# First queries from raw weights, constants inside the planned order, a weight bound by a broadcast product, and transfers counted in flight: one change to a pre-norm transformer block

## The chip, the cores and the metric

The kernel runs on one core of one Trainium2 chip. The metric is the device time of one execution in microseconds (us); lower is better. A core has TensorE (PE in the profile, its weight loads PEld), VectorE (DVE), ScalarE (ACT), GpSimd (POOL) and SyncE (SP), which here only issues transfers. Each engine works through its own instructions in program order and waits where an instruction needs another engine's result.

## The reference

A pre-norm block over one sequence of 2048 tokens of width 640: attention with 32 heads of 20 in a sliding window of 256 keys, then a gated feed-forward of width 1536. All arrays are float32.

```python
def _layernorm(x, axis=-1, eps=1e-5):
    m = jnp.mean(x, axis=axis, keepdims=True)
    v = jnp.var(x, axis=axis, keepdims=True)
    return (x - m) / jnp.sqrt(v + eps)

def _A_ref(x, wqkv, wo):
    H = 32; Dh = D // H; W = 256
    qkv = (x @ wqkv).reshape(B, S, 3, H, Dh).transpose(2, 0, 3, 1, 4)
    q, k, v = qkv[0], qkv[1], qkv[2]
    scores = jnp.einsum("bhqd,bhkd->bhqk", q, k) * (Dh ** -0.5)
    mask = (idx[:, None] - idx[None, :] >= 0) & (idx[:, None] - idx[None, :] < W)
    p = softmax(where(mask, scores, -1e9))
    o = jnp.einsum("bhqk,bhkd->bhqd", p, v)
    return o.transpose(0, 2, 1, 3).reshape(B, S, D) @ wo

def _B_ref(x, w_gate, w_up, w_down):
    return (gelu(x @ w_gate) * (x @ w_up)) @ w_down

h = x + _A_ref(_layernorm(x), wqkv, wo)
h2 = h + _B_ref(_layernorm(h), w_gate, w_up, w_down)
```

## The kernel before

**Precision.** A product of two fp32 matrices is made of three fp16 products: each operand is scaled by a power of two and split into a high and a low half (`xh`, `xl`; `w0h`, `w0l` for the query weights, `w1` for the keys', `w2` for the values'), and high x high, high x low and low x high are summed in PSUM. The power of two of a weight is a bound on its absolute values. `Weight.scale` makes it: a sum or maximum of absolute values per partition into `am`, a product on TensorE that brings all partitions' values to every partition (through `dg`, the identity times `am`, against a matrix of ones), a maximum on VectorE, and bit operations for `pw` (the power) and `sw` (its inverse). `Weight.split` writes the high halves on ScalarE, and `low` the low halves on VectorE.

**Tiles and stages.** The tokens are 16 blocks of 128 and 8 chunks of 256 (two blocks). A block is normalised (`layernorm`, VectorE with a power on GpSimd), transposed on TensorE against `ident`, and split into `xh` and `xl`. `qk(c, 0)` and `qk(c, 1)` make the queries and keys of chunk c: five feature tiles of 128, each a sum over five slices of the inner dimension, three fp16 matmuls of 256 columns for each. Two feature tiles share a PSUM bank (`mm`, two of them); `qk_out` splits the result, writes both halves to DRAM (tile `qk`), and `stack` reads them back into `qT` and `kT`, six transfers each, in the layout in which one matmul covers all three half products of a head pair. Maxima of each row come first (`maxima`, TensorE into `ra` or `rb`, then VectorE into `junk` and `mxs`), then the scores, the exponentials on ScalarE, the windows' edges on GpSimd, and the values on TensorE (`pv`). The output projection, the second normalisation and the feed-forward follow; parts of them run beside the attention of later blocks.

**Storage in the start.** The raw query weights lie in the two buffers that become `qT`; the raw key weights lie in `gu`, which later holds split gate and up weights; blocks 1 to 3 of the input lie in buffers of `pt`. SP issues, in this order: blocks 0 and 1, the five slices of the query weights (`qT<-in_wqkv_dram`), those of the keys (`gu<-in_wqkv_dram`), block 2, the value weights, blocks 3 and 4, then the first slices of the output weights (`wsl`).

**The order of the work.** Nothing is placed by hand. Each piece of work is a generator (a lane); it yields the engine that it needs next and a function that tells when its operands are ready. `Clock` keeps a modelled time for each engine and tile, with a cost for each instruction (`Engine.cost`) and each transfer (`Clock.issue`). The loop at the end looks at the lanes in a fixed preference and emits the next instruction of the first one that can start by the modelled time. So what is emitted, and in what order each engine gets it, follows from the modelled times; on the chip an engine keeps to that order, and waits where its model was too early. When nothing can be emitted and no score has been made yet, a matmul of the fp16 identity into `pv` is emitted, which computes nothing that is used:

```python
            if not pos["score"] and nc.t["tensor"] <= now:
                nc.tensor.matmul(pv[:, 0, :], ident16, ident16, start=True, stop=True)
```

The list order holds from `tc.manual_schedule()` on, which stands just ahead of that loop; what was emitted before it (the identities, the ones, the mask, the memset of `pv`) is placed by the framework's own scheduler.

**What the change touches.** `scale_lane` runs `Weight.scale` for one weight; the keys' waits until the queries' scale is emitted, the values' until the keys' is. `split_lane` splits in the order queries, keys, values, and so on. `big_lane` writes constants into rows of `kT` on GpSimd (12 memsets) once the queries' scale is emitted. `x_lane` normalises and transposes the blocks; from block 2 on it waits for the keys' scale. `dense_lane` picks the next dense product; `can` says whether it may start. In the modelled transfer before, each engine's transfers queue up behind one another (`moved`), and land 3.0 or 3.2 after their last byte was moved:

```python
            self.moved[eng] = max(self.moved[eng], start + 0.2) + cost * (1.2 if run <= 512 else 1)
            end = self.moved[eng] + (3.0 if eng == "sync" else 3.2)
```

Of the kernel before, what the change touches and what calls it, by code (L numbers as in the profile page):

```python
# [53 lines left out]
class Clock:  # L54

    LAT = 0.18
    NOW = ("tensor", "vector", "scalar", "gpsimd", "sync")

    def __init__(self, nc):
        self.nc = nc
        self.t = dict.fromkeys(self.NOW, 0.0)
        self.wr, self.rd, self.rings = {}, {}, {}
        self.warm, self.win, self.use = False, 0, 0.0
        self.mode, self.half = "full", 0
        self.moved = dict.fromkeys(self.NOW, 0.0)
        for e in self.NOW:
            setattr(self, e, Engine(self, e))
# [90 lines left out]
    def issue(self, eng, cost, reads, writes, move=None):  # L160
        start = self.t[eng]
        boxes = [self.box(a) for a in reads], [self.box(a) for a in writes]
        for a, (k, b) in zip(reads, boxes[0]):
            start = max(start, self.latest(self.wr, k, b, eng))
            if a.space == PSUM:
                start = max(start, self.others(a, eng))
        for k, b in boxes[1]:
            start = max(start, self.latest(self.wr, k, b, eng), self.latest(self.rd, k, b, eng))
        if move:
            run = min(b[4] for a, (_, b) in zip(reads + writes, boxes[0] + boxes[1])  # L170
                      if a.space != DRAM)
            self.t[eng] = start + (move if run > 512 else 0.7)
            self.moved[eng] = max(self.moved[eng], start + 0.2) + cost * (1.2 if run <= 512 else 1)
            end = self.moved[eng] + (3.0 if eng == "sync" else 3.2)
        else:
            end = self.t[eng] = start + cost
        for k, b in boxes[0]:
            self.note(self.rd, k, b, eng, end)
        for k, b in boxes[1]:
            self.note(self.wr, k, b, eng, end)  # L180


class Engine:
# [23 lines left out]
    def cost(self, op, out, ins):  # L207
        n = out.free_size()
        if op.startswith("dma_start"):
            size = n * out.partition_size() * mybir.dt.size(out.dtype)  # L210
            return size / (300e3 if mybir.dt.size(out.dtype) == 4 else 150e3)
        half = mybir.dt.size(out.dtype) == 2 and ins and mybir.dt.size(ins[0].dtype) == 2
# [31 lines left out]
def block_kernel(ctx: ExitStack, tc: tile.TileContext, x, wqkv, wo, wg, wu, wd, out):  # L244
# [70 lines left out]


    ident = const.tile([P, P], F32, name="ident")
    nc.vector.memset(ident, 1.0)
# [14 lines left out]
    class Weight:  # L333
# [35 lines left out]
        def scale(self, lane, tp="tp"):  # L369
# [17 lines left out]

            dg = nc.tile(lnp, [P, P], F32, "dg")
            yield on("vector", am)
            nc.vector.tensor_scalar(dg, ident, am[:, 7:8], _pow2(-self.e), op0=ALU.mult, op1=ALU.mult)  # L390
            yield pe(dg, slots=[tp])
            t = bank(tp)
            nc.tensor.matmul(t[:, 0:P], ones, dg, start=True, stop=True)
            pc = pw[:, self.col:self.col + 1]
# [177 lines left out]
    rooms = {"k": gu.bitcast(F32)[:, :KC * D].rearrange("p (c f) -> p c f", f=D)}  # L572
    rooms["k"] = [rooms["k"][:, i] for i in range(KC)]
    gu = gu.rearrange("p (a c f) -> p a c f", c=KC, f=512)

# [36 lines left out]
    esc = const.tile([P, 1], F32, name="esc")  # L612
    hsc = const.tile([P, 1], F32, name="hsc")

    def qk_scale():
# [13 lines left out]
    class Block:  # L629
        ready = False  # L630
        maxima = halves = v = 0
        h, turned, normed = None, False, False
        scored = normal = wrote = 0
# [13 lines left out]
    def x_lane(blocks, lane):  # L647

        for j in blocks:
            c = C[j // 2]  # L650
            if j > 1:
                yield on("vector", when=lambda: W["k" if j < NR else "v"].scaled)
            if j >= NR and j + 1 < NB:
                yield ("sync",), lambda: max(0.0, nc.slot(att, "xt", 2))
                load_x(j + 1)

            def dst():
                if c.x is None:
                    c.x = tuple(nc.tile(wq, [P, KC, CW], F16, n, 3) for n in ("xh", "xl"))
                return tuple(t[:, :, B[j].cols] for t in c.x)  # L660

            yield from layernorm(B[j].x, lane, None, None, dst,
                                 lambda: j < 6 or c.x or C[j // 2 - 3].used == 4,
                                 lambda: B[j].x, tp="rb" if j in (1, 3) else "tp")
            B[j].ready = True

# [8 lines left out]
    def qk(c, which):  # L675

        w = W["qk"[which]]
        xh, xl = C[c].x
        wh, wl = w.hl
        d = dram.tile([2, D, CW], F16, name=f"qk{c}{which}")  # L680
        left = [3]
        for t0 in range(0, KC, 2):
# [11 lines left out]
    def qk_out(c, which, ts, ps, d, left):  # L694

        o = ps[:, :len(ts) * CW].rearrange("p (t n) -> p t n", n=CW)
        yield on("scalar", ps, when=lambda: pos["qk"] < pos["qks"] + 2)
# [5 lines left out]
        nc.vector.scalar_tensor_tensor(lo, o, _pow2(QE), hi, op0=ALU.mult, op1=ALU.subtract)  # L703
        done("mm")
# [618 lines left out]
    def scale_lane(todo, lane):  # L1323
        for i in todo:
# [36 lines left out]
    def dense_lane():  # L1361
# [96 lines left out]

    ctx.enter_context(tc.manual_schedule())
    class Lane:  # L1460
# [11 lines left out]
        def start(self, now):  # L1472
# [43 lines left out]
    while dense.alive or sides or side or outs or tasks:  # L1516
# [8 lines left out]
        ahead = pos["dense"] / DENSE - pos["score"] / (H // 2) - TARGET  # L1525
        early = [l for l in sides if l.gen.__name__ == "x_lane"] if not B[XF].ready else []
        if not W["v"].ready:
# [71 lines left out]
```

## Time and profile before

| | |
|---|---|
| median of 3 runs | 1050.79 us |
| the three runs | 1049.81, 1050.79, 1056.80 us |
| the profiled execution's own time | 1054.5 us |
| its span in the trace | 1052.8 us |
| mean granted TensorE clock | 0.995 of full speed |
| TensorE busy | 1022.7 us, 97% of the span |
| VectorE busy | 777.7 us, 74% |
| ScalarE busy | 489.3 us, 46% |
| GpSimd busy | 266.5 us, 25% |
| first matmul that computes something of the queries | at 22.20 us |
| first matmul of the attention's maxima that waited for keys | at 63.60 us |
| matmuls of the identity into `pv` | 424, until 106.7 us |

Almost every instruction is issued through one helper, so all have line 192 in the profile; groups are told apart by the tiles' names instead. In an instruction's row, `out<-in` are the program's tiles. In a timeline row the first two numbers are start and duration; rows of one kind that follow closely are merged, with their count behind an x, and brackets give the idle time of the engine just before and what ended it. In the chain of waits the columns are start, duration and what was running. In a table of windows each pair is an engine's busy time and number of instructions; behind the pairs stand the granted clock, the share of the DMA engines and GB/s.

### The profile page before, as it was taken

What the parts mean: (1) busy time and instruction counts of PE and PEld (TensorE: products, weight loads), DVE (VectorE), ACT (ScalarE), POOL (GpSimd) and SP (SyncE); (2) the same over time, 40 slices, a digit from 0 to 9 for tenths busy, and PEclk for the clock granted to TensorE, in tenths of its full rate; (3) what the DMA queues carried; (4) which work ended last, traced back from release to release, by engine and by line L of the source; (5) the groups of instructions that cost most, each with busy time, mean ns of one, the idle gap of its engine ahead of it and who ended that gap; (6) DMA issues with size and microseconds to landing.
All of it is one profiled execution on the core that took longest, in us unless ns stands there. A gap on an engine that the chain in (4) does not pass through costs nothing.

```text
span 1052.8 us, 27290 instructions
## 1 busy us (share of the span) xinstructions
PE 1022.7 (97%) x10966; PEld 697.9 (66%) x10966; DVE 777.7 (74%) x2196; ACT 489.3 (46%) x936; POOL 266.5 (25%) x367
## 2 busy tenths in 40 slices
PE   6999899999999999999999999999999999999998
PEld 6977566766766666666655564455777777777776
DVE  5678899998778777666778848576899976555553
ACT  5431566675666666656668763432221222222120
POOL 5000223223323323323334430113434410000000
PEclk9999989999999999999999999999999999999999
DMA  7462445534132231412232224132352471132211
GB/s 288 114 165 55 145 119 118 166 92 105 40 100 80 74 81 40 107 55 77 51 135 76 78 39 162 51 102 75 116 160 100 136 215 59 68 101 101 76 51 50
DMA packets 85727, 105.91 MB, mean 101 GB/s; under 512 B 22944, under 2 KB 59040, under 8 KB 84640
## 3 DMA queue, kind: packets, MB, share of 16 engines
q1 hardware_dynamic: 62496, 93.41, 29.9%
q10 hardware_dynamic: 23104, 10.75, 3.9%
q8 instruction: 86, 1.41, 0.6%
q14 instruction: 41, 0.34, 0.1%
HBM read 71.11 MB, written 28.84 MB: 95 GB/s over the span
## 4 chain that ended last, share of the span: by engine, by line
PE 81%; DVE 10%; ACT 3%; DMA 3%; issue 3%; POOL 1%; SPq 0%; ACTq 0%; DVEq 0%; POOLq 0%
PE mm L192 41%; PE pv L192 12%; PE ra L192 11%; PE rb L192 9%; PE tp L192 7%; DVE junk L192 3%; DMA kT<-qk 1%; ACT pt L192 1%; DMA qk<-qks 1%; DVE am L192 1%; DVE gel L192 0%; DVE gu L192 0%; ACT wst L192 0%; POOL ws L192 0%; DVE ht L192 0%
## 5 line engine op out<-in xcount | busy, mean ns | idle before, releaser
L192 POOL TENSOR_SCALAR_AFFINE_SELECT pt<-pt 128x512 f32<-128x512 f32 x240 | 153.3, 661 | 327.0 <-ACT pt L192 322.6
L192 DVE CUSTOM_DVE_ANT_0 junk<-ra,mask 128x384 bf16<-128x384 f32 (+2 forms) x264 | 140.1, 531 | 41.0 <-PE ra L192 20.9
L192 DVE CUSTOM_DVE_ANT_0 junk<-rb,mask 128x384 bf16<-128x384 f32 (+2 forms) x248 | 131.1, 529 | 43.3 <-PE rb L192 26.0
L192 ACT ACTIVATE pt<-rb,esc 128x384 f32<-128x384 f32 (+2 forms) x246 | 130.1, 581 | 67.3 <-PE rb L192 47.6
L192 ACT ACTIVATE pt<-ra,esc 128x384 f32<-128x384 f32 (+2 forms) x234 | 122.7, 575 | 77.7 <-PE ra L192 68.9
L192 PE MATMUL pv<-pt,v 128*21 128x128 f32 x2880 | 105.0, 277 | 1.0 <-ACT oT L192 0.8
L192 PEld LDWEIGHTS <-ah 128*128 128x128 f16 x768 | 74.9, 98 | 30.2 <-issue 2.9
L192 PEld LDWEIGHTS pv<-pt,v 128*21 128x21 f32 x2880 | 68.8, 101 | 16.0 <-issue 1.8
L192 ACT ACTIVATE gel<-gel,ffk 128x512 f32<-128x512 f32 x32 | 23.1, 722 | 121.0 <-DVE gel L192 116.5
L192 PEld LDWEIGHTS <-kT 62*128 62x128 f16 x1440 | 58.4, 95 | 21.4 <-issue 11.2
L192 ACT CAST ah<-gel 128x512 f16<-128x512 f32 x48 | 29.6, 617 | 82.6 <-DVE gel L192 81.0
L192 PEld LDWEIGHTS <-ws 128*128 128x128 f16 x640 | 62.6, 98 | 7.2
L192 DVE SCALAR_TENSOR_TENSOR ht<-mm,ffk,ht 128x320 f32<-128x320 f32 x96 | 52.0, 545 | 20.6 <-PE mm L192 18.5
L192 PEld LDWEIGHTS <-qT 60*128 60x128 f16 x640 | 24.7, 93 | 63.2 <-issue 59.2
L192 PEld LDWEIGHTS <-gu 128*128 128x128 f16 x440 | 41.8, 98 | 36.9 <-issue 1.5
L192 PE MATMUL mm<-xl,w0h 128*128 128x256 f16 x200 | 54.8, 274 | 0.0
L192 PE MATMUL mm<-xh,w0h 128*128 128x256 f16 x200 | 54.7, 274 | 0.0
L192 PE MATMUL mm<-xl,w1h 128*128 128x256 f16 x200 | 54.7, 273 | 0.0
L192 PE MATMUL mm<-xh,w1l 128*128 128x256 f16 x200 | 54.6, 273 | 0.0
L192 PE MATMUL mm<-xh,w1h 128*128 128x256 f16 x200 | 54.6, 273 | 0.0
L192 PE MATMUL mm<-xh,w0l 128*128 128x256 f16 x200 | 54.6, 273 | 0.0
L192 PE MATMUL mm<-w2h,xh 128*128 128x320 f16 x160 | 48.1, 300 | 0.6 <-DVE qks L192 0.6
(287 smaller groups left out, 2533.5 us busy)
## 6 DMA issues: line engine op xcount, KB each, us to landing
ws<-wsums SPq DMA_DIRECT2D x20, 640.0 KB
qk<-qks ACTq DMA_DIRECT2D x64, 128.0 KB
qT<-qk SPq DMA_DIRECT2D x48, 160.0 KB
kT<-qk SPq DMA_DIRECT2D x48, 160.0 KB
wsums<-ws SPq DMA_DIRECT2D x12, 640.0 KB
ht<-in_x_dram SPq DMA_DIRECT2D x16, 320.0 KB
h_dram<-ht SPq DMA_DIRECT2D x16, 320.0 KB
ht<-h_dram SPq DMA_DIRECT2D x16, 320.0 KB
```

Of the source, the lines that this page charges most:

```text
L192: r = real(*args, **kw)
```

## The change

- **First chunk's queries in fp32.** `qk(0, 0)` multiplies the raw fp32 query weights with the normalised, transposed, unsplit blocks 0 and 1 (new tile `x32`, which lies in `gu` behind the raw key weights), one fp32 matmul of 256 columns for each pair of feature tile and slice. It may start when both blocks are `full` and the query weights' transfers are issued; the power of two is applied in `qk_out` through `qs`. `x_cast` makes `xh` and `xl` of these two blocks afterwards (ScalarE, then GpSimd), once the keys' scale is emitted. The keys are split ahead of the queries, and the stacks of chunks 0 and 1 wait until the query weights are split.
- **Constants inside the list order.** `tc.manual_schedule()` moves ahead of the constants.
- **Weight bound by a broadcast product.** `am`'s column, scaled, is broadcast as the stationary operand against the identity; the diagonal `dg` goes.
- **Transfers in flight.** The order's model of a transfer changes: all engines' transfers share one line, a transfer waits until the eighth before it has landed, the rates and delays are others, and `SAFE` is added to each landing.

```diff
     LAT = 0.18
+    SAFE = 0.5
...
+        self.line, self.window = 0.0, deque(maxlen=8)
...
         if move:
+            if len(self.window) == self.window.maxlen:
+                start = max(start, self.window[0])
             run = min(b[4] for a, (_, b) in zip(reads + writes, boxes[0] + boxes[1])
                       if a.space != DRAM)
-            self.t[eng] = start + (move if run > 512 else 0.7)
-            self.moved[eng] = max(self.moved[eng], start + 0.2) + cost * (1.2 if run <= 512 else 1)
-            end = self.moved[eng] + (3.0 if eng == "sync" else 3.2)
+            self.t[eng] = start + (0.35 if run > 512 else 0.75)
+            out = writes[0].space == DRAM
+            self.line = max(self.line, self.t[eng] + (0.3 if out else 1.1)) + cost
+            end = self.line + (0.9 if out else 1.1) + self.SAFE
+            self.moved[eng] = self.line
+            self.window.append(end)
...
         if op.startswith("dma_start"):
-            size = n * out.partition_size() * mybir.dt.size(out.dtype)
-            return size / (300e3 if mybir.dt.size(out.dtype) == 4 else 150e3)
+            size = math.prod(c for _, c in out.ap) * mybir.dt.size(out.dtype)
+            if op == "dma_start_transpose":
+                return size / 150e3
+            wide = mybir.dt.size(out.dtype) == 4 or out.space == DRAM
+            return size / (380e3 if wide else 150e3)
...
+    ctx.enter_context(tc.manual_schedule())
     ident = const.tile([P, P], F32, name="ident")
...
-            dg = nc.tile(lnp, [P, P], F32, "dg")
             yield on("vector", am)
-            nc.vector.tensor_scalar(dg, ident, am[:, 7:8], _pow2(-self.e), op0=ALU.mult, op1=ALU.mult)
-            yield pe(dg, slots=[tp])
+            nc.vector.tensor_scalar(am[:, 7:8], am[:, 7:8], _pow2(-self.e), None, op0=ALU.mult)
+            yield pe(am, slots=[tp])
             t = bank(tp)
-            nc.tensor.matmul(t[:, 0:P], ones, dg, start=True, stop=True)
+            nc.tensor.matmul(t[:, 0:P], am[:, 7:8].to_broadcast([P, P]), ident, start=True,
+                             stop=True)
...
+    x32 = gu.bitcast(F32)[:, KC * D:KC * (D + CW)].rearrange("p (c n) -> p c n", n=CW)
...
             def dst():
-                if c.x is None:
-                    c.x = tuple(nc.tile(wq, [P, KC, CW], F16, n, 3) for n in ("xh", "xl"))
-                return tuple(t[:, :, B[j].cols] for t in c.x)
+                if j < 2:
+                    return x32[:, :, B[j].cols], None
+                return xparts(j)
...
-            B[j].ready = True
+            if j < 2:
+                B[j].full = True
+                tasks.append(x_cast(j))
+            else:
+                B[j].ready = True
+
+    def xparts(j):
+        c = C[j // 2]
+        if c.x is None:
+            c.x = tuple(nc.tile(wq, [P, KC, CW], F16, n, 3) for n in ("xh", "xl"))
+        return tuple(t[:, :, B[j].cols] for t in c.x)
+
+    def x_cast(j):
+        src = x32[:, :, B[j].cols]
+        yield on("scalar", src, when=lambda: W["k"].scaled)
+        hi, lo = xparts(j)
+        nc.scalar.copy(hi, src)
+        yield on("gpsimd", hi)
+        nc.gpsimd.tensor_tensor(lo, src, hi, op=ALU.subtract)
+        B[j].ready = True
...
+                if first:
+                    yield from products(KC, lambda k: [(w.raw[0, k][:, fs], x32[:, k, :])],
+                                        at_=(ps, i * CW))
+                    continue
...
+        up = qs if c == which == 0 else _pow2(QE)
+        yield on("scalar", ps, when=lambda: pos["qk"] < pos["qks"] + 2 and (c or pos["qs"]))
...
-        nc.scalar.activation(hi, o, AF.Copy, scale=_pow2(QE))
+        nc.scalar.activation(hi, o, AF.Copy, scale=up)
...
-        yield ("sync",), need(d, when=lambda: pos["big"] == 2 and (c < 2 or B[2 * c - 3].scored),
-                              eng="sync")
+        yield ("sync",), need(d, when=lambda: pos["big"] == 2 and (W["q"].ready if c < 2 else
+                                                                B[2 * c - 3].scored), eng="sync")
...
+            if i == 0:
+                yield on("vector", sw)
+                nc.vector.tensor_scalar(qs, sw[:, C_Q:C_Q + 1], _pow2(QE), None, op0=ALU.mult)
+                pos["qs"] = 1
...
-        for i, w in enumerate(weights):
+        for i, w in [(1, weights[1]), (0, weights[0]), *enumerate(weights)][:2] + list(
+                enumerate(weights))[2:]:
...
+            if f is qk and i == which[0] == 0:
+                return B[1].full and W["q"].loaded
...
-    ctx.enter_context(tc.manual_schedule())
     class Lane:
...
-                back = EARLY if not B[XF].ready else LATE
+                back = EARLY if not B[XF].full else LATE
```

More of the change, by code (lines that the diff above doesn't have):

```diff
@@ L613, in block_kernel @@
     hsc = const.tile([P, 1], F32, name="hsc")
+    qs = const.tile([P, 1], F32, name="qs")
     def qk_scale():
@@ L631, in block_kernel @@
         maxima = halves = v = 0
-        h, turned, normed = None, False, False
+        h, turned, normed, full = None, False, False, False
         scored = normal = wrote = 0
@@ L677, in qk @@
         w = W["qk"[which]]
-        xh, xl = C[c].x
-        wh, wl = w.hl
+        first = c == which == 0
+        if not first:
+            xh, xl = C[c].x
+            wh, wl = w.hl
         d = dram.tile([2, D, CW], F16, name=f"qk{c}{which}")
@@ L696, in qk_out @@
         o = ps[:, :len(ts) * CW].rearrange("p (t n) -> p t n", n=CW)
-        yield on("scalar", ps, when=lambda: pos["qk"] < pos["qks"] + 2)
+        up = qs if c == which == 0 else _pow2(QE)
+        yield on("scalar", ps, when=lambda: pos["qk"] < pos["qks"] + 2 and (c or pos["qs"]))
         pos["qk"] += 1
@@ L700, in qk_out @@
         hi, lo = (st[:, i, :len(ts), :] for i in range(2))
-        nc.scalar.activation(hi, o, AF.Copy, scale=_pow2(QE))
+        nc.scalar.activation(hi, o, AF.Copy, scale=up)
         yield on("vector", hi, after=ps)
-        nc.vector.scalar_tensor_tensor(lo, o, _pow2(QE), hi, op0=ALU.mult, op1=ALU.subtract)
+        nc.vector.scalar_tensor_tensor(lo, o, up, hi, op0=ALU.mult, op1=ALU.subtract)
         done("mm")
@@ L1525, in block_kernel @@
         ahead = pos["dense"] / DENSE - pos["score"] / (H // 2) - TARGET
-        early = [l for l in sides if l.gen.__name__ == "x_lane"] if not B[XF].ready else []
+        early = [l for l in sides if l.gen.__name__ == "x_lane"] if not B[XF].full else []
         if not W["v"].ready:
```

## The prediction

> **What bounds the kernel now.** I read the page first, then the chain of waits, then the start of the timeline engine by engine, then the windows.
>
> ```profile
> span 1052.8 us, 27290 instructions
> PE 1022.7 (97%) x10966; PEld 697.9 (66%) x10966; DVE 777.7 (74%) x2196; ACT 489.3 (46%) x936; POOL 266.5 (25%) x367
> PE 81%; DVE 10%; ACT 3%; DMA 3%; issue 3%; POOL 1%; SPq 0%; ACTq 0%; DVEq 0%; POOLq 0%
> L192 PE MATMUL pv<-ident 128*128 128x128 f16 x424 | 30.4, 230 | 6.2 <-DVE ident L192 6.2
> ```
>
> TensorE sets the time. But its 97% is flattered: the 424 matmuls of the last row, a group of the first 110 us, compute nothing. The order writes them where TensorE would idle before the first scores. So a change gains where it removes idle time or these fillers, and the start holds most of both.
>
> ```profile
> 1.25 0.29 POOL L192 TENSOR_SCALAR_AFFINE_SELECT ident<-ident 128x128 f32<-128x128 f32 x1
> 1.32 0.48 DVE L192 MEMSET pv<- 128x512 f32 x1
> 5.91 0.21 DVE L192 CAST ident<-ident 128x128 f16<-128x128 f32 x1
> 6.18 5.99 PE L192 MATMUL pv<-ident 128*128 128x128 f16 x59 [6.18 <-DVE ident L192]
> 6.67 0.61 DVE L192 TENSOR_SCALAR xt<-xt,lmvx,lyx 128x640 f32<-128x640 f32 x1
> 8.00 0.68 DVE L192 TENSOR_SCALAR pt<-pt,lmvxb,lyxb 128x640 f32<-128x640 f32 x1
> 12.01 0.61 PE L192 MATMUL tp<-ident,xt 128*128 128x128 f32 x4
> 12.65 0.58 ACT L192 CAST xh<-tp 128x512 f16<-128x512 f32 x1 [3.99 <-PE tp L192]
> 15.21 0.29 ACT L192 CAST xh<-rb 128x128 f16<-128x128 f32 x1
> 16.45 2.24 DVE L192 TENSOR_SCALAR dg<-ident,am 128x128 f32<-128x128 f32 x1
> 20.90 4.07 DVE L192 SCALAR_TENSOR_TENSOR w0l<-qT,sw,w0h 128x640 f16<-128x640 f32 x5 [0.77 <-ACT w0h L192]
> 22.20 0.27 PE L192 MATMUL mm<-xh,w0h 128*128 128x256 f16 x1
> ```
>
> Two things hold the first useful product to 22.20. Block 0 is normalised at 7.28 (6.67 + 0.61), but its transposes start at 12.01: fillers stand before them in TensorE's queue, and the fillers began only at 6.18, because the fp16 identity was cast at 5.91 though its input was ready at 1.54. Then the query weights go through maximum, bound, split.
>
> **The change part by part.**
>
> Constants in the order: the cast of the identity then stands right behind the select (end 1.54), and fillers can start after the memset of pv (up to 0.21 + 0.48 later, some 2.4). The first 59 now end at 12.17 (6.18 + 5.99); a start 3.8 earlier ends them near 8.4. No instruction is added; what hid the late cast was nothing, TensorE idled 6.18.
>
> First queries in fp32: 25 products of 256 columns replace 75 in fp16. Prices:
>
> ```profile
> 48.60 0.24 PE ra L192 x2
> 19.23 3.13 PE pv L192 x56
> 22.36 0.33 PE mm L192 x3
> 7.83 0.74 ACT L192 ACTIVATE w0h<-qT 128x640 f16<-128x640 f32 x1 [0.81 <-DMA qT<-in_wqkv_dram]
> 14.33 0.75 ACT L192 ACTIVATE w0h<-qT 128x640 f16<-128x640 f32 x1
> 14.97 0.20 ACT L192 ACTIVATION_READ_ACCUMULATOR w0h<-qT 128x1 f32 x1
> 6.00:12.00 6.00, 5.82 (x59) 5.82 (x60) 2.46 (x11) 1.66 (x4) 5.30 (x6) 1.00 1.02 397
> ```
>
> In the chain an fp32 product of 128 columns takes 0.24 (first row), an fp16 one 3.13/56 = 0.056: about four times. [...] Queries of chunk 0: 25 x 0.44 = 11.0 (10.7 to 12.0) against 75 x 0.11 = 8.3, so 2.7 more TensorE work.
>
> They start when both blocks stand in x32 and the raw slices are in. Block 1 is normalised at 8.68; four transposes (some 0.5), the 0.58 copy, the two short copies of 0.29 end near 10.5. Slices: ScalarE waited for the second until 7.83; at 397 GB/s a slice of 320 KB takes 0.83, so the fifth is in near 7.83 + 3 x 0.83 = 10.3. I take a start at 11.0 (10.5 to 12.0), and an end at 22.0.
>
> Before, the same queries end near 32.7, since they also waited for the low halves slice by slice (the 4.07 row). So 10.7 is gained there, the 2.7 already paid.
>
> ```profile
> 25.94 0.16 DVE L192 TENSOR_REDUCE am<-am 128x1 f32<-128x6 f32 x1 [0.97 <-ACT w1h L192]
> 27.76 0.83 ACT L192 ACTIVATE w1h<-gu,sw 128x640 f16<-128x640 f32 x1 [1.86 <-DVE sw L192]
> 28.70 0.87 DVE L192 SCALAR_TENSOR_TENSOR w1l<-gu,sw,w1h 128x640 f16<-128x640 f32 x1
> 32.75 1.34 PE pv L192 x24
> L192 POOL TENSOR_TENSOR w10l<-wst,w10h 128x640 f16<-128x640 f32 x2 | 2.8, 1402 | 3.2 <-ACT wst L192 3.2
> 41.98 0.29 DVE L192 TENSOR_TENSOR xl<-rb,xh 128x128 f16<-128x128 f32 x1 [0.89 <-ACT xh L192]
> 44.01 0.27 PE L192 MATMUL mm<-xh,w0h 128*128 128x256 f16 x1
> ```
>
> What is late next is k. Its maxima still wait for q's scale. ScalarE from 7.83: four more |q| sums at 0.84 each with their read (14.33 to 15.17), and 1.7 of copies, to 12.9; the chain from sum to scale is 27.76 - 25.94 = 1.8, so 14.7; five |k| sums 4.2, to 18.9; the chain again, 20.7; now k is split first: 0.83 + 0.87, first low half at 22.4, just behind q's end at 22.0. The fifth follows at 22.4 + 4 x 0.87 = 25.9, four more feature tiles at 15 x 0.11 end near 32.5. Chunk 1's queries need blocks 2 and 3 and the query split, which moves behind k's: 5 x 0.83 on ScalarE from 24.9, low halves to 30. Blocks 2 and 3 were ready 42.27 - 27.76 = 14.5 after k's first split; the same distance from 20.7 gives 35.2, a quick one 32.5. Against 44.01 before that is 8.8 to 11.5; **I take 10.**
>
> The rest of the move: x_cast adds two ScalarE copies (0.75 each, as 128x640 in the rows) and two GpSimd subtractions, and takes four subtractions from VectorE. GpSimd's rows bound them: 1.40 for a 128x640 subtraction; GpSimd is 25% busy, and its readers, keys of chunk 0, come behind 22. If that cover went, key products would start up to 1.4 later. The query stack now waits for the query split near 30 (qT lies over the raw weights); the key stack, behind it on SP, waits for key products that end near 32.5 and is the later one, so I cost it at nothing; uncovered, six query transfers would push the keys' by up to the 10.41 that six issues took (next fence).
>
> Bound by a broadcast product: 13 diagonals at 0.29 become single-column operations at 0.15: 1.8 of VectorE over the kernel, hidden behind TensorE. The diagonal in the start took 2.24 and ended, at 18.69, just as GpSimd was through with its memsets of kT:
>
> ```profile
> 7.38 11.22 POOL L192 MEMSET kT<- 32x1024 f32 x12
> L192 DVE TENSOR_SCALAR dg<-ident,am x13: 278/286/2241, 16.4 to 710.7; 128x128 f32<-128x128 f32 x13
> L192 DVE TENSOR_SCALAR lvex<-lmvx 128x1 f32<-128x1 f32 x3 | 0.5, 154 | 0.1
> 63.60 0.27 PE L192 MATMUL rb<-kT,qT 60*128 60x128 f16 x3 [2.16 <-DMA kT<-qk]
> 48.68 10.41 SPq L192 DMA_DIRECT2D kT<-qk  x6
> 44.00:108.00 64.00, 12.29 (x179) 0.00 (x0) 0.00 (x0) 0.00 (x0) 1.00 0.48 118
> ```
>
> The new operation costs between 0.15 and those 2.24; k's first low half comes at 22.4 or 24.5. I take the first, as it is nearest to the one-column rows beside it; with the other the 10 becomes 8. [...]
>
> Transfers counted in flight: this adds no instruction; it moves all. Nothing in this trace shows the new order, so I bound it: fillers from 44 to 108 are 179 x 0.056 = 10.0, with the wait of 2.16 at 63.6 that is 12.2 at most to win there (keys of chunk 0 ready earlier bring scores earlier, and the fillers stop); to lose, the third rival's price. I take a gain of 2: there the order already had work on most of TensorE, and what feeds it still passes ScalarE and VectorE.
>
> Sum: 10 + 2 = 12. The profiled execution took 1054.5 (span 1052.8 and 1.7 around it), so 1042.5 by its count. It stands 3.7 above the median of the three runs, 1050.79; the same 12 off the median gives **1039**. Its own range, with 8 to 11.5 in the start and -2 to 5 behind it, is 1034 to 1045.
>
> **The rivals.**
>
> First, the fillers behind 44 go as well. For it: TensorE has the products of chunk 1 from 33 to 50, and keys could land before 50 instead of 63.5. Against: VectorE and ScalarE carry the value weights' split in the same stretch. It gives 10 + 12.2 = 22, so 1029.
>
> Second, VectorE becomes the bound behind the start:
>
> ```profile
> 160.00:260.00 100.00, 96.26 (x1305) 66.14 (x1297) 91.02 (x304) 64.47 (x132) 30.10 (x48) 1.00 0.46 120
> 108.00:160.00 52.00, 47.05 (x566) 29.62 (x569) 45.97 (x150) 31.98 (x66) 14.04 (x22) 0.93 0.45 130
> ```
>
> VectorE (third pair) is 88 to 91% busy where maxima and scores run together, and TensorE's idle time there is 8.7. If the lead is spent waiting for VectorE, two thirds of it go: a gain of 4, 1047. Against it: VectorE's maxima start earlier too, and until 63.60 it has none to do.
>
> Third, slower: keys are planned too early. By the code's figures the old order reckoned six stack transfers at 0.2 + 6 x 1.31 + 3.0 = 11.1, the new one at 0.75 + 1.1 + 6 x 1.09 + 1.6 = 10.0; from first issue to TensorE's start they took 63.60 - 48.68 = 14.9. TensorE works in order, so maxima written too early hold all behind them.
>
> ```profile
> PE rb L192 <- DMA kT<-qk: 3.8, 2, 1.9
> 130.00:140.00 10.00, 7.68 (x95) 4.40 (x95) 9.57 (x28) 7.38 (x14) 2.52 (x4) 0.72 0.40 128
> ```
>
> Behind 108 that wait comes twice, 1.9 at the longest, and the granted clock falls beside such gaps (0.72; 0.93 over 52 us is 3.6). So a wait costs 1.9 + 1.8 = 3.7 now and 4.8 with 1.1 more. In all seven later chunks that is 33.6, less the 7.4 already paid: 26 lost, 1065. It decides from four chunks on, where 19.2 - 7.4 meets the gain of 12. Against: two of seven do it today, and the limit on transfers in flight puts others later, not earlier.
>
> Fourth, the start doesn't move: the order still writes as many fillers before the transposes that these end near 12. Then queries start as copies end, near 15.5, and finish 6.1 earlier than before: 1044.7.
>
> **How the numbers follow.** A measurement of this kernel tells about 1% (10.5) from no change. Chances: forecast 0.50, first rival 0.20, second 0.13, third 0.12, fourth 0.05. Of the forecast's own range three fifths lie under 1040.3: 0.30, and with the first rival 0.50 faster. Within 1%: the other 0.20, the second, the fourth and a quarter of the third, 0.41. Slower: 0.09. The range takes the first rival in whole, to 1028, and above reaches past the second, to 1053.
>
> **What would show it.** First fillers near 2.4 instead of 6.18; the transposes near 8; the first fp32 product of raw weight and x32 near 11, fifty instructions at about 0.22 apart; k's first split near 21; fewer fillers by about half of 424; first maxima near 50 instead of 63.6. Behind 160 TensorE's busy share should stay at 96% and over. Wrong it is if maxima start no earlier than 60, if waits for kT come in four chunks or more, or if the windows of 108 to 260 lose more than 12 to idle time and clock.

## The result and the profile after

| kernel | median | lowest to highest | ratio to before |
|---|---|---|---|
| before | 1051.24 us | 1049.81 to 1056.8 (4 runs) | 1 |
| after | 1064.65 us | 1063.76 to 1069.7 (4 runs) | 1.0125 [1.0094, 1.0157] |

The change made the kernel slower by 1.25%, 13.4 us, where 1039 and a gain of 12 were predicted; it lies outside the predicted range, which ended at 1053. The profiled execution after took 1064.57, 10.1 more in its span than before. The page of after: the span, the busy times, the chain of waits by engine.

```profile
span 1062.9 us, 27135 instructions
PE 1028.4 (97%) x10876; PEld 695.8 (65%) x10876; DVE 776.8 (73%) x2193; ACT 490.6 (46%) x938; POOL 270.9 (25%) x369
PE 75%; DVE 12%; DMA 5%; ACT 3%; issue 3%; POOL 1%; ACTq 0%; SPq 0%; DVEq 0%; POOLq 0%
```

The shares of busy time are as before to a percent. What differs is the chain: TensorE has 75% of it instead of 81%, VectorE and the transfers have 2 points more each. The chain now leaves TensorE more often, and the page doesn't say where.

**The start went nearly as predicted.** Rows of after's timeline, in order of time (start, duration, engine, line, operation; in brackets the idle time before it and who ended it):

```profile
2.52 5.87 PE L199 MATMUL pv<-ident 128*128 128x128 f16 x66 [2.52 <-DVE pv L199]
7.04 11.56 POOL L199 MEMSET kT<- 32x1024 f32 x12
7.15 1.18 DVE L199 TENSOR_SCALAR xt<-xt,lmvx,lyx 128x640 f32<-128x640 f32 x1
8.48 0.63 PE L199 MATMUL tp<-ident,xt 128*128 128x128 f32 x4
11.38 0.15 DVE L199 TENSOR_SCALAR am<-am 128x1 f32<-128x1 f32 x1
11.92 4.48 PE L199 MATMUL mm<-gu,qT 128*128 128x256 f32 x20
16.46 6.64 PE L199 MATMUL mm<-gu,qT 128*128 128x256 f32 x30
18.86 0.83 ACT L199 ACTIVATE w1h<-gu,sw 128x640 f16<-128x640 f32 x1 [0.50 <-DVE qks L199]
25.41 0.27 PE L199 MATMUL mm<-xh,w1h 128*128 128x256 f16 x1 [1.02 <-DVE qks L199]
36.20 1.34 PE L199 MATMUL pv<-ident 128*128 128x128 f16 x21
37.81 0.27 PE L199 MATMUL mm<-xh,w0h 128*128 128x256 f16 x1 [0.28 <-ACT xh L199]
56.25 0.29 DVE L199 CUSTOM_DVE_ANT_0 junk<-rb,mask 128x128 bf16<-128x128 f32 x1 [6.88 <-PE rb L199]
```

The fillers start at 2.52, the transposes at 8.48, the fp32 queries near 11.9 and end at 23.10; the keys are split from 18.86. Chunk 1's queries begin at 37.81 (44.01 before), VectorE's maxima at 56.25 (63.87 before).

**The loss lies between 80 and 120.** First the fillers of both kernels, then both kernels' windows: the stretch, its length, busy time of PE, PEld, DVE, ACT and where shown POOL, granted clock, DMA share, GB/s. In the first fence are before's 80 to 100 and 100 to 120, then before's tile `pv` in 80 to 100; the second has the same three rows of after.

```profile
L192 PE MATMUL pv<-ident x424: 219/219/314, 6.2 to 106.7; 128*128 128x128 f16 x142
80.00:100.00 20.00, 20.00 (x184) 14.29 (x184) 17.10 (x78) 3.05 (x6) 0.00 (x0) 1.00 0.23 58
100.00:120.00 20.00, 17.77 (x164) 11.47 (x163) 16.02 (x54) 6.34 (x17) 2.46 (x4) 1.00 0.50 149
80.00:100.00 20.00, 0.95 (x11) 0.00 (x0) 0.00 (x0) 0.00 (x0) 1.00 0.23 58
```

```profile
L199 PE MATMUL pv<-ident x359: 219/219/311, 2.5 to 100.6; 128*128 128x128 f16 x180
80.00:100.00 20.00, 19.95 (x187) 12.43 (x185) 16.44 (x68) 3.07 (x8) 0.00 (x0) 1.00 0.03 7
100.00:120.00 20.00, 13.66 (x154) 6.86 (x151) 17.76 (x57) 11.65 (x25) 6.59 (x10) 0.73 0.52 160
80.00:100.00 20.00, 5.21 (x84) 0.00 (x0) 0.00 (x0) 0.00 (x0) 1.00 0.03 7
```

From 80 to 100 both kernels' TensorE is full, but in after 5.21 of it are fillers against 0.95: 4.3 less work. From 100 to 120 it is 13.66 busy at a clock of 0.73 against 17.77 at 1.00: 10.0 against 17.8. Fillers in it are 0.84 in after and 1.74 in before, so 9.1 against 16.0 of useful work, 6.9 less. Together 11.2.

Over the whole run I use one measure, the **lead**: the matmul rows of a trace that started before a moment, fillers left out, less the same sum of before. Each row is priced by its columns and type, at the spacing that such rows have in after (0.109 for 256 columns in fp16, 0.216 for one of the two instructions that make 256 columns in fp32, 0.027 for a value product; the two rows that run side by side in maxima and scores at half each: in before's chain of waits four of 128 columns take 0.11 at 63.87). With the fp32 queries there is 2.7 more work to do, so such a kernel's lead shows 2.7 more than it has in time. After leads by 8.2 at 20 us, 7.4 at 40, 4.0 at 60, 8.5 at 80, 2.9 at 100, -5.2 at 120; then it stays near -7 (-8.2 at 200, -5.9 at 260, -5.7 at 620, -7.4 at 1020). The last, less the 2.7, is the 10.1 of the span. The start's gain is there, and it is gone by 120.

**What is missing there is dense work, and block 5 is why.** From the timelines, before first: VectorE's statistics of block 5 and TensorE's first query product of chunk 2. Then, all of after: the second half of block 4's statistics, its high half on ScalarE and its low half on VectorE; block 5's statistics; TensorE's last dense product before the gap, three of the four rows of fillers, the first dense product behind it; SP's issues, and the longest entry of SP's waits in the window 80 to 125.

```profile
57.48 0.88 DVE L192 BATCH_NORM_STATS2 lstx<-xt 128x6 f32<-128x320 f32 x2
83.85 0.28 PE L192 MATMUL mm<-xh,w0h 128*128 128x256 f16 x1
```

```profile
42.40 0.48 DVE L199 BATCH_NORM_STATS2 lstx<-xt 128x6 f32<-128x320 f32 x1
47.93 0.58 ACT L199 CAST xh<-tp 128x512 f16<-128x512 f32 x1 [0.51 <-PE tp L199]
58.12 0.69 DVE L199 TENSOR_TENSOR xl<-tp,xh 128x512 f16<-128x512 f32 x1
102.63 0.88 DVE L199 BATCH_NORM_STATS2 lstx<-xt 128x6 f32<-128x320 f32 x2
92.83 0.30 PE L199 MATMUL mm<-w2h,xl 128*128 128x320 f16 x1
93.42 1.07 PE L199 MATMUL pv<-ident 128*128 128x128 f16 x16
95.02 2.41 PE L199 MATMUL pv<-ident 128*128 128x128 f16 x40
98.88 1.96 PE L199 MATMUL pv<-ident 128*128 128x128 f16 x32
119.98 0.39 PE L199 MATMUL mm<-xh,w0h 128*128 128x256 f16 x1
41.19 0.36 SPq L199 DMA_DIRECT2D xt<-in_x_dram  x1
73.31 0.51 SPq L199 DMA_DIRECT2D ht<-in_x_dram  x1
99.99 0.63 SPq L199 DMA_DIRECT2D xt<-in_x_dram  x1
SPq L199 <- DVE m L199: 24.8, 1, 24.8
```

Block 4 has its statistics by 42.40 in after, block 5 only at 102.63, 60 later, though its load was issued at 41.19. In before it stood at 57.48, ahead of the first maxima. Chunk 2's queries need blocks 4 and 5: they begin at 119.98 instead of 83.85, and from 93.13 (92.83 + 0.30) to 119.98, 26.9 us, TensorE has no dense product: 96 fillers between maxima, then maxima, scores, values and transposes alone, which wait for VectorE and ScalarE. SP is no help: behind 73.81 its next issue waits 24.8, and block 6's load follows at 99.99.

The code says how this comes about. In the loop the maxima's VectorE halves (`max_out`, in `outs`) stand ahead of `x_lane` (in `sides`), and once the value weights are split they may be put on VectorE while it is modelled up to 0.75 ahead; `x_lane` only up to 0.4 (`LATE`). So from the moment that maxima keep VectorE booked, `x_lane` gets no turn. In before block 5's statistics came through just ahead of that moment. In after the maxima start 7.6 earlier, and block 5 missed it. Block 4 is caught first, and the lane takes block 5 after it: its high half is done at 48.51 (47.93 + 0.58), its low half follows only at 58.12, behind the first maxima. On the chip VectorE is idle for 6.88 just ahead of these (the 56.25 row), since its list has them next and they wait for keys. This reading is the theory that the experiments test; its main rivals are that one of the four parts costs the time by itself, above all that keys are now planned too early (the prediction's third rival).

### The profile page after: what moved, and what is told of

The parts are those of the page before. It is cut to its first block, busy times and chain, and to the rows that moved or that the text cites. A ratio compares the mean times of both kernels' runs of the same rounds, so it can differ in the third digit from the quotient of the medians.

```text
span 1062.9 us, 27135 instructions
## 1 busy us (share of the span) xinstructions
PE 1028.4 (97%) x10876; PEld 695.8 (65%) x10876; DVE 776.8 (73%) x2193; ACT 490.6 (46%) x938; POOL 270.9 (25%) x369
## 4 chain that ended last, share of the span: by engine, by line
PE 75%; DVE 12%; DMA 5%; ACT 3%; issue 3%; POOL 1%; ACTq 0%; SPq 0%; DVEq 0%; POOLq 0%
PE mm L199 39%; PE ra L199 11%; PE pv L199 10%; PE rb L199 9%; PE tp L199 7%; DVE junk L199 4%; DMA qk<-qks 2%; ACT pt L199 2%; DVE m L199 1%; DVE xt L199 1%; DMA wst<-in_wg_dram 1%; POOL ws L199 0%; DMA wst<-in_wd_dram 0%; DVE qks L199 0%; DVE am L199 0%
## 5 line engine op out<-in xcount | busy, mean ns | idle before, releaser
L199 DVE CUSTOM_DVE_ANT_0 junk<-rb,mask 128x384 bf16<-128x384 f32 (+2 forms) x266 | 141.2, 531 | 54.8 <-PE rb L199 32.8
L199 ACT ACTIVATE pt<-ra,esc 128x384 f32<-128x384 f32 (+2 forms) x250 | 131.8, 580 | 76.5 <-PE ra L199 62.6
L199 DVE CUSTOM_DVE_ANT_0 junk<-ra,mask 128x384 bf16<-128x384 f32 (+2 forms) x246 | 130.0, 528 | 38.3 <-PE ra L199 17.9
L199 ACT ACTIVATE pt<-rb,esc 128x384 f32<-128x384 f32 (+2 forms) x230 | 121.0, 578 | 56.6 <-PE rb L199 44.0
L199 PE MATMUL rb<-kT,qT 60*128 60x384 f16 (+2 forms) x336 | 45.1, 291 | 6.3 <-DMA kT<-qk 2.7
L199 PE MATMUL mm<-xh,w0h 128*128 128x256 f16 x175 | 48.2, 275 | 1.7 <-DVE qks L199 1.4
L199 PE MATMUL mm<-xl,w0h 128*128 128x256 f16 x175 | 48.2, 276 | 0.5 <-DVE xl L199 0.5
```

Source lines behind the costliest of these rows:

```text
L199: r = real(*args, **kw)
```

## The experiments

Each ratio is to before run on the same chip, with its 95% interval (before's median was 1051.24 to 1056.0 in the four sets of runs, so only ratios are compared). "Block 5" and "chunk 2" are the start of block 5's statistics and of chunk 2's queries in that kernel's timeline.

| run | ratio | block 5 | chunk 2 |
|---|---|---|---|
| after | 1.0125 [1.0094, 1.0157] | 102.63 | 119.98 |
| a_first5 | 0.9994 [0.9973, 1.0016] | 62.70 | 82.57 |
| b_hold5 | 1.0210 [1.0187, 1.0233] | 108.98 | 128.06 |
| b_bcast | 1.0226 [1.0201, 1.0251] | 112.44 | 121.53 |
| a_nofp32 | 1.0010 [0.9992, 1.0028] | 44.98 | 76.80 |
| a_oldmodel | 1.0126 [1.0085, 1.0167] | 104.44 | 122.00 |
| b_bcast_pin | 1.0142 [1.0105, 1.0178] | 54.99 | 84.28 |
| b_const | 0.9968 [0.9943, 0.9993] | 51.86 | 80.28 |
| b_fp32 | 0.9943 [0.9920, 0.9967] | 50.72 | 76.43 |
| b_fp32_const | 0.9947 [0.9927, 0.9967] | 48.55 | 79.38 |
| b_model | 1.0085 [1.0060, 1.0109] | 48.11 | 79.84 |
| a_first5_oldmodel | 0.9933 [0.9915, 0.9952] | 46.75 | 76.46 |
| a_safe1_pin | 0.9964 [0.9942, 0.9986] | 49.67 | 80.35 |

**Block 5 first, in after (a_first5).** The preference that `x_lane` has for the first blocks is held until block 5 is ready.

```diff
-                back = EARLY if not B[XF].full else LATE
+                back = EARLY if not B[5].ready else LATE
-        early = [...x_lane...] if not B[XF].full else []
+        early = [...x_lane...] if not B[5].ready else []
```

> The changed kernel; only the preference for the lanes that normalise blocks now holds until block 5 is ready, not just until block 1. Theory (the change loses because block 5 is normalised behind the maxima, so that TensorE runs out of dense products near 93 us): block 5 is normalised before 75 us instead of from 102.6, the fillers of 93 to 100 us go, and the time falls by 12 to 20 from 1064.7, to 1045 to 1053. Rival (VectorE is the bound of the first attention blocks and takes any lead away): within 4 of the changed kernel, 1060 to 1068, with the maxima later by what the normalisation took.

0.9994: the 1.25% of loss is gone with all four parts in place. Timelines of VectorE and TensorE, and the windows 100 to 120:

```profile
62.70 0.88 DVE L199 BATCH_NORM_STATS2 lstx<-xt 128x6 f32<-128x320 f32 x2
82.57 0.27 PE L199 MATMUL mm<-xh,w0h 128*128 128x256 f16 x1
100.00:120.00 20.00, 18.18 (x174) 11.54 (x174) 18.01 (x55) 10.06 (x24) 4.35 (x7) 1.00 0.52 163
```

TensorE is 18.18 busy at full clock where after had 13.66 at 0.73; the lead at 120 is 3.7 instead of -5.2. It has its price: at 80 the lead is 3.9, where after had 8.5. The edit moves blocks 2 to 4 as well, so it is the lane's turn, not one instruction, that is shown.

**Block 5 late, in before (b_hold5).** In `x_lane`, block 5 is held until 41 pairs of maxima are in the order, as in after's order. The blocks behind it, which the same lane makes, follow later too.

```diff
+            if j == 5:
+                yield on("vector", when=lambda: pos["max"] >= 41)
```

> The kernel before; only the normalisation of block 5 is held back until 41 pairs of maxima are in the order, where the changed kernel has it. Theory: TensorE starves as in the changed kernel between 90 and 120 us, 10 to 20 slower than before, 1061 to 1071. Rival (VectorE bound): within 4 of 1051.

1.0210, without any part of the change. Its timeline and windows:

```profile
108.98 0.48 DVE L192 BATCH_NORM_STATS2 lstx<-xt 128x6 f32<-128x320 f32 x1
128.06 0.28 PE L192 MATMUL mm<-xh,w0h 128*128 128x256 f16 x1
80.00:120.00 40.00, 36.59 (x351) 21.03 (x349) 34.74 (x132) 15.99 (x35) 7.09 (x11) 0.84 0.22 69
```

The same gap opens, with a clock of 0.84, and the lead is -8.2 at 120 and -14.0 at 200; a second piece (-12 to -20) goes between 340 and 620. The cause of that later loss is open.

**The broadcast product alone (b_bcast)**, the part with the least work in it, put into before.

```diff
...
-            nc.vector.tensor_scalar(dg, ident, am[:, 7:8], _pow2(-self.e), op0=ALU.mult, op1=ALU.mult)
...
-            nc.tensor.matmul(t[:, 0:P], ones, dg, start=True, stop=True)
+            nc.vector.tensor_scalar(am[:, 7:8], am[:, 7:8], _pow2(-self.e), None, op0=ALU.mult)
...
+            nc.tensor.matmul(t[:, 0:P], am[:, 7:8].to_broadcast([P, P]), ident, start=True, stop=True)
```

> The kernel before with the broadcast product alone (one small VectorE operation in place of a diagonal, 13 times). The planned order has block 5 behind 41 pairs of maxima here too. Theory: slower by 8 to 20, 1059 to 1071, though nothing of its own costs anything. Rival (the loss comes from fp32 queries or from the model of transfers): 1047 to 1053.

1.0226, the slowest of all, from thirteen operations that each became shorter (in the median 0.286 in before and 0.153 in after).

```profile
112.44 0.88 DVE L192 BATCH_NORM_STATS2 lstx<-xt 128x6 f32<-128x320 f32 x2
121.53 0.40 PE L192 MATMUL mm<-xh,w0h 128*128 128x256 f16 x1
```

Block 5 is late again; the lead is -0.8 at 100 and -12.6 at 120. So a small shift in the modelled times is enough to put block 5 on the wrong side of the edge; the start's gain isn't needed for that.

**After without the fp32 queries (a_nofp32):** that part undone, the other three kept.

```diff
-                if first:
-                    yield from products(KC, lambda k: [(w.raw[0, k][:, fs], x32[:, k, :])],
-                                        at_=(ps, i * CW))
-                    continue
...
-        for i, w in [(1, weights[1]), (0, weights[0]), *enumerate(weights)][:2] + list(
-                enumerate(weights))[2:]:
+        for i, w in enumerate(weights):
```

> The changed kernel without its first part: queries of chunk 0 in fp16 as before, the other three parts kept. The planned order has block 5 early, at 6 pairs of maxima. Theory: no loss, 1040 to 1052 (the earlier fillers bring the first transposes forward by some 4). Rival (the model of transfers is at fault): 1058 to 1068.

1.0010: the loss is gone here too, but nothing is gained. Block 5 comes at 44.98 and the lead at 120 is 6.5, although the queries start later; it is spent by 260 (-2.5).

**After with the old transfer model (a_oldmodel):** the part "transfers counted in flight" undone.

```diff
...
-            self.line = max(self.line, self.t[eng] + (0.3 if out else 1.1)) + cost
-            end = self.line + (0.9 if out else 1.1) + self.SAFE
+            self.moved[eng] = max(self.moved[eng], start + 0.2) + cost * (1.2 if run <= 512 else 1)
+            end = self.moved[eng] + (3.0 if eng == "sync" else 3.2)
...
```

> The changed kernel with the old model of transfers: part four undone, the other three kept. The planned order still has block 5 behind 48 pairs of maxima. Theory (place of block 5): still slow, 1.008 to 1.022 of the kernel before. Rival (the new model of transfers is what costs the time): 0.985 to 1.003.

1.0126, as after: the loss of 80 to 120 does not need the new model. Block 5 is late (104.44), the lead -6.0 at 120 and -5.5 at 340 (-7.5 in after). That the whole times agree so well is in part chance: two further losses (380 to 440 and 620 to 700) bring the lead to -16.4 at 1020. They are not explained; the profiled execution was also the longest of the four, 5.4 above their median.

**Broadcast product with the lane first (b_bcast_pin):** b_bcast, and `x_lane` held first until block 5, up to 1.0 ahead.

```diff
+                back = 1.0 if not B[5].ready else LATE
+        early = [...x_lane...] if not B[5].ready else []
```

> The kernel before with the broadcast product, and the lanes that normalise blocks put first, with VectorE's modelled time allowed 1.0 ahead, until block 5 is ready. The planned order has block 5 ahead of the first maxima. Theory: of the 1.0226 that the broadcast product alone measured at least two thirds go: 0.994 to 1.008. Rival (the broadcast product costs the time itself, by a slow weight load or a longer chain): 1.015 to 1.025.

1.0142, between the two expectations and in neither, though the interval reaches into the rival's. Block 5 is early (54.99) and the lead at 120 -0.3, so the gap of 93 to 120 is cured; but it falls to -9.4 at 200 and -14.1 at 340. So **block 5's place is not the only place where this order can lose 1%**; what loses it here is open. That the broadcast product costs it by itself fits badly: a_first5_oldmodel below has that product and stands at 0.9933, b_fp32_const does not have it and stands at 0.9947.

**The other parts alone**: the constants (`tc.manual_schedule()` moved up), the fp32 queries, both, and the new transfer model, each put into before as the change has it.

> The kernel before with its constants inside the order: part two alone. The planned order is the same, so only the start moves: fillers from 2.5 us, transposes near 8 instead of 12. ScalarE has the copies then ahead of its sums, so the queries' scale comes 0 to 4 earlier. Theory: 0.996 to 1.001. If the start passes through in full (4 us): 0.996.

> The kernel before with the first part alone: queries of chunk 0 in fp32, keys split first. The planned order has block 5 early, at 4 pairs of maxima. Its constants still come late, so the first product starts near 15, not 11.8: 7 earlier than before, for 2.7 more work of TensorE. Theory: a lead of 4, 0.994 to 1.002. Rival (fp32 queries cost more than they bring, by the weight loads or what they push back on ScalarE): 1.006 to 1.02.

> Parts one and two together (fp32 queries, constants inside the order), without the broadcast product and with the old model of transfers. Its planned order is that of part one alone, with block 5 early. Theory: the two gains are in one place, the start, and each measured 0.9943 and 0.9968; together 0.988 to 0.996, the fastest so far. Rival (the gains do not add, the lead is given back behind 100 us): 0.994 to 1.003.

> The kernel before with the new model of transfers alone: part four. The planned order has block 5 early, at 6 pairs of maxima. Theory (no part costs anything where block 5 is early): 0.995 to 1.008. Rival (the new model makes TensorE wait for kT): 1.008 to 1.02, with waits for kT of over 8 us behind 108 us in place of 3.8.

The constants alone gain 0.3% (0.9968), the fp32 queries 0.6% (0.9943), each with block 5 early; their leads at 120 are 2.9 and 6.6. Together they give 0.9947, which lies in both expected ranges, and is no more than the fp32 queries alone: the gains don't add, and why is open. The model alone costs 0.85% (1.0085) with block 5 early (48.11), so there is a second loss that block 5's place doesn't explain. Its longest wait for keys on TensorE between 108 and 640, and its windows:

```profile
PE ra L199 <- DMA kT<-qk: 4.5, 1, 4.5
200.00:360.00 160.00, 152.51 (x2139) 103.40 (x2137) 123.80 (x413) 98.24 (x201) 47.52 (x76) 0.98 0.31 80
```

With a second wait of 1.0 that makes 5.5, against 3.8 in before: not the 8 that the rival of this run expected, nor waits in several chunks as the prediction's third rival had it. The ratio lies in that rival's range, but the lead falls from 4.7 at 120 to -5.7 at 340, by far more than the 1.7 between the waits.

**Block 5 first and the old model (a_first5_oldmodel); block 5 first and a slower model (a_safe1_pin).** a_first5 leads by 5.0 at 200 and no longer at 340 (-0.2). If the new model plans keys too early there, either of these keeps the lead. The first is after with the edits of a_first5 and a_oldmodel; the second has `SAFE` doubled and holds the lane first as in b_bcast_pin, up to 1.0 ahead (a_first5: 0.6).

```diff
-    SAFE = 0.5
+    SAFE = 1.0
...
-                back = EARLY if not B[XF].full else LATE
+                back = 1.0 if not B[5].ready else LATE
...
```

> The changed kernel with block 5 first and the old model of transfers. The planned order has block 5 ahead of all maxima. It tells whether the lead that the run with block 5 first lost between 220 and 340 us went to the new model's early maxima. Theory: it keeps that lead, 0.985 to 0.997. Rival (the lead is lost in any order, to VectorE): 0.997 to 1.005.

> The changed kernel with SAFE at 1.0 instead of 0.5 (each landing planned 0.5 later) and the normalising lanes first, with VectorE's modelled time allowed 1.0 ahead, until block 5 is ready; block 5 is planned at 6 pairs of maxima. Theory: with block 5 early and keys planned later 0.988 to 1.000. Rival (the new model costs the lead whatever SAFE is): 1.000 to 1.012.

0.9933 and 0.9964: both beat before, and the first is the fastest kernel of the study, 0.7% under before and about 2% under after. TensorE's waits for keys (108 to 640) and windows, first of a_first5, then of a_first5_oldmodel:

```profile
PE rb L199 <- DMA kT<-qk: 4.6, 2, 2.6
PE ra L199 <- DMA kT<-qk: 1.4, 1, 1.4
200.00:360.00 160.00, 153.75 (x2168) 104.18 (x2167) 125.79 (x428) 100.14 (x205) 46.70 (x76) 0.98 0.28 74
```

```profile
PE ra L192 <- DMA kT<-qk: 1.0, 1, 1.0
200.00:360.00 160.00, 158.22 (x2296) 108.66 (x2296) 126.70 (x434) 102.96 (x211) 50.73 (x83) 1.00 0.31 81
```

With the old model TensorE is 158.22 of 160 busy at full clock, with the new one 153.75 at 0.98: 4.5 of idle time and 3.2 (0.02 x 160) of clock. The waits for keys are 6.0 against 1.0. Its lead stays (7.1 at 200, 9.0 at 340, 10.4 at 1020); that of a_safe1_pin stays to 340 (8.5 at 200, 9.4 at 340) and ends at 6.6. That keys planned too early are the whole of this second loss is argued, not shown: both runs also have block 5 earlier (46.75 and 49.67 against 62.70), and with the model the whole order changed.

Four runs set the two mechanisms side by side:

| | block 5 late | block 5 early |
|---|---|---|
| new transfer model | 1.0125 (after) | 0.9994 (a_first5) |
| old transfer model | 1.0126 (a_oldmodel) | 0.9933 (a_first5_oldmodel) |

Block 5's place is worth 1.3 to 1.9%. The model is worth 0.6% where block 5 is early; that it is worth nothing where block 5 is late isn't shown, since a_oldmodel has its two later losses besides.

## Why the prediction was wrong

**The step that failed** is the term of 2 for transfers counted in flight, with its reason "there the order already had work on most of TensorE, and what feeds it still passes ScalarE and VectorE". It priced 44 to 108 by the fillers that could go, as if the order there stayed what it was. What feeds it did pass VectorE: block 5, and in the new order it came 45 later. Where +2 (bounds -2 to 5) stood, 80 to 120 alone cost 11.2 by the windows, 13.7 by the lead. In time (the lead less the 2.7) after was 5.8 ahead at 80 and 10.1 behind at the end: of the 22.1 between the gain of 12 and this loss, 4.2 are the start's (5.8 instead of 10) and 17.9 are this term's. All parts emit into one list, so each can move this; the prediction charged the reordering to one part, which is not needed for the loss (a_oldmodel, 1.0126, is without it).

**The reason against the second rival was the wrong way round.** "VectorE's maxima start earlier too, and until 63.60 it has none to do" named an empty VectorE as cover. That empty time was where blocks 4 and 5 were normalised. With the maxima 7.6 earlier in the list, the rows behind them were shut out. Nor was it the rival itself, VectorE as the bound: VectorE is 16.44 of 20 busy from 80 to 100, less than before's 17.10. From 100 to 120 it is busier, 17.76, but a_first5 has 18.01 there and a TensorE that is 18.18 busy at full clock. It was a matter of turn, not of capacity.

**The third rival's sign was right, its mechanism is not what happened.** It wanted waits for `kT` in four chunks or more and 1065. The time came out at 1064.65 by another way, so that the numbers agree is luck. After waits for keys once, for chunk 0, and behind 108 not at all, where before has the 3.8 of the prediction's row:

```profile
55.98 0.27 PE L199 MATMUL rb<-kT,qT 60*128 60x128 f16 x3 [2.70 <-DMA kT<-qk]
```

It may have a part in the 0.6% between a_first5 and a_first5_oldmodel.

**The start's term had the right mechanism and was too large.** Against the steps:

- Fillers near 2.4, transposes near 8, first fp32 product near 11, fifty at 0.22: 2.52, 8.48, 11.92, and 6.64/30 = 0.22. The end at 23.10 instead of 22.0. No row of before shows the 0.44 for one fp32 product, which is four times the 0.11 of an fp16 one, nor the 10.7 as the least for 25; in after two instructions 0.216 apart make one, 0.43, and the 25 take 11.2 (11.92 to 23.10). The fourth rival, that the start doesn't move, is out.
- The bound by a single column: 0.15 at 11.38, under memsets of `kT` on GpSimd (7.04 to 18.60): the lower of its two ends, as taken. Why a single column isn't held up there, where before's diagonal took 2.24, no run shows.
- k's first split near 21: 18.86, earlier. But the key products began at 25.41, since the bank had to be emptied by VectorE, whose copies of the queries' low halves stood behind k's own low halves.
- Chunk 1's queries at 35.2 at the latest: 37.81, behind fillers, waiting for `xh`. So 6.2 was gained there, not 8.8 to 11.5, and by the lead at 80 us 8.5 - 2.7 = 5.8, not 10.
- First maxima near 50 instead of 63.6: 55.98. Fillers fewer by about half of 424: fewer by 65, 359 are left.
- Behind 160 TensorE at 96% and over: 94.87 of 100 busy from 160 to 260, 98% from 160 to the end.

Of the signs named for being wrong one came true, the one on the windows: 108 to 260 should lose no more than 12 to idle time and clock. The windows of before and after:

```profile
108.00:260.00 152.00, 143.31 (x1859) 95.77 (x1862) 136.99 (x452) 96.44 (x197) 44.14 (x70) 0.98 0.46 124
```

```profile
108.00:260.00 152.00, 140.05 (x1786) 93.14 (x1782) 130.73 (x426) 91.48 (x185) 43.18 (x66) 0.96 0.44 119
```

After, the second row, loses 12.0 to idle time and 6.1 to the clock (0.04 x 152), 18 in all; before lost 8.7 and 3.0.

**The range** failed for the same reason as the sum. It was made of prices of parts. b_hold5, with no work added or taken away, moved the time by 2.1% through the order alone, almost the width of the whole range given (2.4%).

**What stays open:** why b_bcast_pin loses behind 120, what the new model's loss is made of, why the constants and the fp32 queries don't add, and the later losses of a_oldmodel and b_hold5. No run singles them out. Of after's own 10.1 in the span, the stretch of 80 to 120 accounts for the turn from gain to loss: from 5.8 at 80 to -7.9 at 120 (the lead less the 2.7). The remaining 2 come in small pieces behind it, and are not traced to a cause.

## What to carry to other kernels

Where a loop writes the order from modelled times and fixed preferences, a change that moves the start moves the whole list: before pricing the parts, ask of each rarely served lane what lets it through, and whether work that now begins earlier will shut it out. Such a lane shows in a trace as one instruction whose input landed long ago (here some 60 us), followed by a stretch in which TensorE has no product of its main stream; fillers in that stretch hide it from the busy shares. A version with the feeder's turn pinned tells the order's accident from the price of the change: here it took the loss back (0.9994), and with the old transfer model it brought 0.7%.

## What the runs showed of the hardware

Some of VectorE's wide operations took longer beside GpSimd's. After's normalisation of block 0 took 1.18 under the memsets of `kT` (0.61 before, ahead of them). The stretch varies: block 1's took 0.68 under them in before and 0.95 in after. In before that row began at 8.00, late in a memset of 0.94, and the next memset took 1.29, so there the waiting may have been GpSimd's. The low halves of k, beside the two subtractions that the change gives to GpSimd, took 2.98 for two, and 1.66 for two right behind them. The subtractions took 3.34 for two, where the prediction had 1.40 for one:

```profile
18.68 3.34 POOL L199 TENSOR_TENSOR xl<-gu,xh 128x640 f16<-128x640 f32 x2
19.72 2.98 DVE L199 SCALAR_TENSOR_TENSOR w1l<-gu,sw,w1h 128x640 f16<-128x640 f32 x2 [0.32 <-ACT w1h L199]
23.04 1.66 DVE L199 SCALAR_TENSOR_TENSOR w1l<-gu,sw,w1h 128x640 f16<-128x640 f32 x2
```

So, if the stretch is GpSimd's doing, the subtractions that were taken off VectorE cost it 1.3 again. And the stretch in which TensorE starves cost twice here: in after's 100 to 120 its busy time is 4.1 less than before's, and the granted clock is 0.73 besides.
